# Sliding-window attention feeding an ELU feed-forward block on one core: x turned by DMA instead of by TensorE, and the attention pairs begun two steps sooner

## The chip, the core and the metric

The kernel runs on one core of a Trainium2 chip. The core has five engines with instruction streams of their own, and they meet only through semaphores: TensorE (PE, with its weight loads shown apart as PEld), VectorE (DVE), ScalarE (ACT), GpSimd (POOL) and SyncE (SP). Here SP does nothing but issue DMAs. The metric is device microseconds of one execution. A profiled execution has a span, from its first instruction to its last, which is a little shorter than its time.

## What is computed

```python
# attention, per batch b and head h: B=8, H=8, S=576, D=64
scores = scale * q @ k.T
scores = where(|i - j| <= 32, scores, -1e9)
attn   = exp(scores - max) / sum            # softmax over j
x      = attn @ v                           # -> (B*S, H*D) = (4608, 512)
# feed-forward, w_in (512, 2048), w_out (2048, 512)
h   = x @ w_in
g   = where(h > 0, h, exp(min(h, 0)) - 1)   # ELU
out = g @ w_out                             # (4608, 512)
```

## The kernel before

**Units of work.** The 4608 rows of x are cut into 36 pairs. A pair `i` is two blocks of 64 query rows, 128 rows in all, with all eight heads. Two pairs make a tile `t` of 256 rows for the feed-forward block, 18 tiles in all; pair `2t` is its first half, pair `2t+1` its second. The feed-forward work of a tile is eight steps of two slices of 128 hidden features each, so there are 144 steps, numbered `kk`. From the third tile on, tile `t` has steps 8t to 8t+7.

**A step.** The loop at the end of the kernel writes each step's work out in a fixed order, and each engine runs its own part of that order: `elu` of the step before (DVE, L446); the tasks in slot "dve"; `mm1` (eight PE matmuls, L433, the exponential on ACT, L439, and a subtraction on DVE, L441); the tasks in slot "mid"; `mm2` of two steps before (four PE matmuls, L460); the tasks in slot "end". After a tile's last step `mm2` also copies the result out of PSUM, half on ACT (L468) and half on DVE (L469), and stores it by SP (L470).

**A pair.** `pair_at(i, kk)` places the stages of one pair: `scores` (16 PE matmuls, L252, and an exponential on ACT, L258) in "mid" of step kk; `mask` (DVE, L267) and `pv` (16 PE matmuls, L279) in step kk+1; `normalize` (DVE, L288 and L291, which writes `x_st`) in "dve" of step kk+2 and `x_transpose` (four PE transposes into PSUM, L300) at its "end"; `x_evac` (DVE copy of PSUM to `xT`, L310) in "dve" of step kk+3. From pair 8 on kk is 4(i-2). So for the second half of tile t the four stages lie in steps 8t-4 to 8t-1, and `mm1` of step 8t, which reads both halves of `xT[t]`, comes next. Scores, attention output and transposed x share one PSUM buffer, tag "s".

**q, k and v.** For each batch b, SP loads q and k as f32 (`load_qk`, L109, 1152 KB each), POOL casts a quarter at a time (`cast_qk`, L207), PE transposes it (`transpose_qk`, L229, six transposes, PSUM tag "t0") and ACT copies it to `qT` or `kT` (L205). POOL loads v (`load_v`, L118), and SP makes a copy of it shifted by 64 rows with two DMAs (`rotate_v`, L124 and L125). The first step of the batch is `k0` = 4(9b//2 - 2). Batch 2 has its quarters transposed in steps 20 to 27, cast two steps ahead; a later batch has them in every second step from k0-15 on, cast five steps ahead. `rotate_v` is placed in step k0-4, the loads in steps k0-32 and k0-31 (not before 18), and `load_v` two steps after.

**Queues.** SP takes its DMAs strictly in the order of the loop, and one that has to wait keeps those behind it. The SP sequence is loads of q and k, shifts of v and stores of results. The pool of `xT` has three buffers, that of `x_st` two.

Of the kernel before, what the change touches and what calls it, by code (L numbers as in the profile page):

```python
# [10 lines left out]
BF16 = mybir.dt.bfloat16  # L11
# [10 lines left out]
def kernel(  # L22
# [9 lines left out]
    nc = tc.nc  # L32
# [11 lines left out]
    HP = H // 2  # L44
# [6 lines left out]
    TT = 256  # L51
    NT = N_TOK // TT
    NDO = D_MODEL // 128
# [3 lines left out]
    HALF = STEPS // 2  # L57
# [5 lines left out]
    wpool = ctx.enter_context(tc.tile_pool(name="weights", bufs=1))  # L63
    lpool = ctx.enter_context(tc.tile_pool(name="loads", bufs=2))
    apool = ctx.enter_context(tc.tile_pool(name="attn", bufs=2))
    xpool = ctx.enter_context(tc.tile_pool(name="xT", bufs=3))
    mpool = ctx.enter_context(tc.tile_pool(name="moe", bufs=3))
    opool = ctx.enter_context(tc.tile_pool(name="outs", bufs=2))

# [15 lines left out]
    def ps_tile(shape, dt, tag, name):  # L85
        return pools[tag].tile(shape, dt, tag=tag, name=name)
# [79 lines left out]
    for m in (1, 2, 0, 3, 4):  # L166
# [10 lines left out]
        out=masks, in_=masks, compare_op=ALU.is_ge, fill=0.0,  # L177
        base=0, pattern=[[0, 5], [-1, QB]], channel_multiplier=1)
    nc.gpsimd.affine_select(
        out=masks, in_=masks, compare_op=ALU.is_ge, fill=0.0,  # L180
        base=2 * WIN, pattern=[[0, 5], [1, QB]], channel_multiplier=-1)
    for mi in (0, 4):
        nc.gpsimd.affine_select(
            out=masks[:, mi, :], in_=masks[:, mi, :], compare_op=ALU.is_ge,
            fill=0.0, base=-WIN, pattern=[[0, QB]], channel_multiplier=1)
    nc.gpsimd.affine_select(
        out=masks[:, 3, :], in_=masks[:, 3, :], compare_op=ALU.is_ge,
# [55 lines left out]
    st = {}  # L243
# [59 lines left out]

    xT = {}

    def x_evac(i):
        t, z = i // 2, i % 2
        if z == 0:
            xT[t] = xpool.tile([128, NDO, TT], BF16, tag="xT", name="xT")
        nc.vector.tensor_copy(xT[t][:, :, z * 128:(z + 1) * 128], st.pop(i))  # L310

    def first_pair(b):
        return NQB * b // 2
# [20 lines left out]
    for fn in (pv, normalize, x_transpose, x_evac):  # L334
        for i in (0, 1):
            fn(i)
# [26 lines left out]
    def at(kk, slot, fn, *args):  # L363
        tasks.setdefault((kk, slot), []).append((fn, args))
# [5 lines left out]
    def pair_at(i, kk):  # L370
        at(kk, "mid", scores, i)
        at(kk + 1, "dve", mask, i)
        at(kk + 1, "end", pv, i)
        at(kk + 2, "dve", normalize, i)
        at(kk + 2, "end", x_transpose, i)
        at(kk + 3, "dve", x_evac, i)


    for i, tag in ((2, "s"), (3, "u")):
        at(0, "mid", scores, i, tag)  # L380
        at(1, "dve", mask, i)
        at(1, "mid", pv, i)
        at(2, "dve", normalize, i)
        at(2, "mid", x_transpose, i)
        at(3, "dve", x_evac, i)
# [11 lines left out]
    pair_at(6, 18)  # L397
    pair_at(7, 21)
    for i in range(8, NPAIR):
        pair_at(i, HALF * (i - 2))  # L400
    for b in range(2, B):
        k0 = HALF * (first_pair(b) - 2)
        for n in range(2 * HP):
            if b == 2:
                which, hp, kk, ahead = n // HP, n % HP, 20 + n, 2
            else:
                which, hp, kk, ahead = n % 2, n // 2, k0 - 15 + 2 * n, 5
            at(kk - ahead, "mid", cast_qk, b, which, WHOLE, (hp,), nc.gpsimd)
            at(kk, "mid", transpose_qk, b, which, WHOLE, (hp,), nc.scalar)
        at(k0 - HALF, "mid", rotate_v, b)  # L410
        if b >= 3:
            kk = max(k0 - 8 * HALF, 18)
            at(kk, "mid", load_qk, b, 0, WHOLE)
            at(kk + 1, "mid", load_qk, b, 1, WHOLE)
            for m in range(VS):
                at(kk + 2 + m // 3, "mid", load_v, b, m)
# [8 lines left out]
    def mm1(kk):  # L425
        t, s = order[kk]
        h = kk % 2 if kk < 18 else (kk + 2) % 3
        ps = ps_tile([128, FG, TT], FP32, f"h{h}", "ps")
        psH[kk] = ps
        for j in range(FG):  # L430
            fo = s * FG + j
            for do in range(NDO):
                nc.tensor.matmul(  # L433
                    ps[:, j, :],
                    lhsT=w_in_sb[:, do, fo * 128:(fo + 1) * 128],
                    rhs=xT[t][:, do, :],
                    start=(do == 0), stop=(do == NDO - 1))
        e_sb = mpool.tile([128, FG, TT], FP32, tag="e_sb")
        nc.scalar.activation(e_sb, ps, AX.Exp)  # L439
        m_sb = mpool.tile([128, FG, TT], BF16, tag="m_sb")  # L440
        nc.vector.tensor_scalar(m_sb, e_sb, -1.0, None, ALU.add)  # L441
        m_t[kk] = m_sb
# [30 lines left out]
    for kk in range(NSTEP + LAG):  # L473
        run(kk, "first")
        if 1 <= kk <= NSTEP:
            elu(kk - 1)
        run(kk, "dve")
        if kk < NSTEP:
            mm1(kk)
        run(kk, "mid")  # L480
        if kk >= LAG:
            mm2(kk - LAG)
        run(kk, "end")
# [30 lines left out]
```

## Time and profile before

| | |
|---|---|
| median of 3 runs | 351.5 us (351.49 to 351.5) |
| profiled execution, its own time | 352.11 us |
| its span | 350.4 us |
| PE busy | 314.8 us |
| DVE busy | 256.2 us |
| ACT busy | 167.2 us |
| POOL busy | 84.2 us |
| granted TensorE clock | 1.0 throughout |

Rows of the trace give a start and a length in us from the span's start, the engine, the line and the operation with its output and inputs. Where a row ends in brackets, it tells how long the engine was idle before it and what it waited for. Successive matmuls overlap in such rows, so the cost of a group of matmuls is read from one start to the next, not from the lengths.

### The profile page before, as it was taken

The numbers are of one execution on the slowest core, as the hardware profiler recorded it, in microseconds if no ns is written. First come the engines' busy times: TensorE is split into PE (matmuls) and PEld (weight loads), VectorE is DVE, ScalarE is ACT, GpSimd is POOL, SyncE is SP. The second block draws the span as 40 slices with busy tenths as digits, with TensorE's granted clock in tenths as the row PEclk, the third lists the DMA queues.
The fourth block names the chain that finished last, engine by engine and source line by source line (L and its number), as shares of the span: only waits on it lengthen the run. The fifth ranks groups of instructions, "written<-read, shape, count | busy, mean of one in ns | idle before, by whom it ended". The sixth has DMA issues, their size and how long they took to land.

```text
span 350.4 us, 8157 instructions
## 1 busy us (share of the span) xinstructions
PE 314.8 (90%) x3356; PEld 212.4 (61%) x3408; DVE 256.2 (73%) x474; ACT 167.2 (48%) x262; POOL 84.2 (24%) x108
## 2 busy tenths in 40 slices
PE   0347999688999999999999999999999999999994
PEld 0335666455666666666666566666666666666662
DVE  4456667786888777888777877778877777777763
ACT  2524273734645553545454554454545454444331
POOL 8432310282842304212601604031100000000000
PEclk9999999999999999999999999999999999999999
DMA  8999999999999739703939494950103010101011
GB/s 177 187 232 212 217 162 209 214 279 201 148 232 160 73 68 206 146 0 107 85 105 226 82 101 72 227 161 6 62 2 117 7 62 0 62 2 61 2 60 60
DMA packets 63944, 42.00 MB, mean 120 GB/s; under 512 B 38564, under 2 KB 58020, under 8 KB 63908
## 3 DMA queue, kind: packets, MB, share of 16 engines
q1 hardware_dynamic: 22180, 32.58, 38.8%
q0 software_dynamic: 41728, 8.92, 35.2%
q8 instruction: 26, 0.43, 0.5%
q14 instruction: 10, 0.08, 0.1%
HBM read 36.70 MB, written 9.44 MB: 132 GB/s over the span
## 4 chain that ended last, share of the span: by engine, by line
PE 73%; DVE 14%; ACT 4%; DMA 4%; issue 3%; SPq 0%; DVEq 0%
PE ps L433 32%; PE psY L460 28%; PE ptx L229 4%; DVE g_sb L446 4%; PE psS L252 3%; DVE x_st L291 3%; PE psXT L300 3%; PE psS L279 3%; ACT e_sb L439 3%; DVE m_sb L441 2%; DMA f<-in_k_dram 2%; DVE y_sb L469 2%; DMA Vo<-Ve 2%; DVE pm L267 2%; ACT pu L258 1%
## 5 line engine op out<-in xcount | busy, mean ns | idle before, releaser
L439 ACT ACTIVATE e_sb<-ps 128x512 f32<-128x512 f32 x144 | 86.0, 597 | 163.7 <-PE ps L433 163.6
L433 PE MATMUL ps<-xT,w_in_sb 128*128 128x256 bf16 x1152 | 150.7, 274 | 4.2 <-DVE xT L310 3.3
L460 PE MATMUL psY<-w_out_sb,g_sb 128*128 128x512 bf16 x524 | 141.0, 379 | 3.0 <-DVE g_sb L446 0.2
L433 PEld LDWEIGHTS <-w_in_sb 128*128 128x128 bf16 x1152 | 109.1, 98 | 34.7 <-issue 4.8
L441 DVE TENSOR_SCALAR m_sb<-e_sb 128x512 bf16<-128x512 f32 x144 | 72.0, 500 | 59.9 <-ACT e_sb L439 59.5
L446 DVE SCALAR_TENSOR_TENSOR g_sb<-ps,m_sb 128x512 bf16<-128x512 f32 x144 | 99.4, 690 | 13.0
L460 PEld LDWEIGHTS <-g_sb 128*128 128x128 bf16 x576 | 50.7, 97 | 38.0 <-DVE g_sb L446 0.7
L207 POOL CAST qkb<-f 96x768 bf16<-96x768 f32 x48 | 41.8, 889 | 110.1 <-DMA f<-in_q_dram 49.7
L118 POOL DMA_DIRECT2D Ve<-in_v_dram x40 | 34.1, 860 | 48.6 <-PE psS L279 34.6
L229 PE MATMUL ptx<-ident,qkb 96*128 96x96 bf16 x384 | 27.6, 215 | 14.5 <-DVE qkb L207 12.1
L258 ACT ACTIVATE pu<-psS 128x1024 bf16<-128x1024 f32 x36 | 36.4, 1018 | 1.8 <-PE psS L252 1.7
L229 PEld LDWEIGHTS <-qkb 96*128 96x128 bf16 x384 | 23.6, 102 | 16.8 <-DVE qkb L207 12.6
L267 DVE TENSOR_TENSOR pm<-pu,masks 128x1024 bf16<-128x1024 bf16 x36 | 27.8, 773 | 2.3 <-ACT pu L258 2.1
L291 DVE TENSOR_TENSOR x_st<-psS,rc 128x512 bf16<-128x512 f32 x36 | 24.9, 692 | 1.2
L279 PEld LDWEIGHTS <-pm 128*64 128x64 bf16 x576 | 12.5, 113 | 17.7 <-issue 8.1
L205 ACT COPY qT<-ptx 128x576 bf16<-128x576 bf16 (+1 forms) x30 | 20.0, 666 | 4.2 <-PE ptx L229 4.2
L300 PEld LDWEIGHTS <-x_st 128*128 128x128 bf16 x144 | 9.6, 99 | 16.5 <-DVE x_st L291 14.3
L300 PE MATMUL psXT<-ident,x_st 128*128 128x128 bf16 x144 | 14.6, 225 | 4.1 <-DVE x_st L291 3.6
L205 ACT COPY kT<-ptx 128x576 bf16<-128x576 bf16 (+1 forms) x26 | 17.4, 670 | 0.0
L279 PE MATMUL psS<-Ve,pm 128*64 128x65 bf16 x320 | 16.5, 200 | 0.6 <-ACT pu L258 0.3
L279 PE MATMUL psS<-Vo,pm 128*64 128x65 bf16 x256 | 14.5, 201 | 2.7 <-DMA Vo<-Ve 1.9
L252 PE MATMUL psS<-qT,kT 64*128 64x64 bf16 x576 | 15.3, 196 | 1.7 <-DVE xT L310 1.0
(29 smaller groups left out, 84.0 us busy)
## 6 DMA issues: line engine op xcount, KB each, us to landing
out_dram<-y_sb SPq DMA_DIRECT2D x18, 512.0 KB, 3.0
f<-in_q_dram SPq DMA_DIRECT2D x6, 1152.0 KB, 11.7
f<-in_k_dram SPq DMA_DIRECT2D x6, 1152.0 KB, 15.8
Vo<-Ve SPq DMA_DIRECT2D x12, 260.0 KB, 4.3
Ve<-in_v_dram POOLq DMA_DIRECT2D x24, 128.0 KB, 13.7
f<-in_q_dram SPq DMA_DIRECT2D x4, 576.0 KB, 9.6
f<-in_k_dram SPq DMA_DIRECT2D x4, 576.0 KB, 11.9
w_in_sb<-in_moe_w_in_dram POOLq DMA_DIRECT2D x4, 512.0 KB, 18.8
```

What stands on the lines that cost most here:

```text
L205: nc.scalar.copy(d_, s_)
L207: eng.tensor_copy(d_, s_)
L229: nc.tensor.transpose(pt[:, g, j * SP_:(j + 1) * SP_], src[:, j, g * 128:(g + 1) * 128], ident[0:SP_, 0:SP_])
L258: nc.scalar.activation(pu, _bap(psS, [psS.ap[0], [1, 1024]]), AX.Exp, scale=SCALE)
L267: nc.vector.tensor_mul(pm, pu, _bap(mm, [mm.ap[0], [0, H], [1, 2 * QB]]))
L279: nc.tensor.matmul(psS[QB * z:QB * (z + 1), par, hp * VD:(hp + 1) * VD], lhsT=pm[:, par * HP + hp, z * QB:(z + 1) * QB], rhs=vv[:, qb // 2 ...
L291: nc.vector.tensor_mul(x_st, _bap(psS, [psS.ap[0], [VD, HP], [512, 2], [1, D]]), _bap(rc, [rc.ap[0], [2, HP], [1, 2], [0, D]]))
L433: nc.tensor.matmul(ps[:, j, :], lhsT=w_in_sb[:, do, fo * 128:(fo + 1) * 128], rhs=xT[t][:, do, :], start=(do == 0), stop=(do == NDO - 1))
L439: nc.scalar.activation(e_sb, ps, AX.Exp)
L441: nc.vector.tensor_scalar(m_sb, e_sb, -1.0, None, ALU.add)
L446: nc.vector.scalar_tensor_tensor(g_sb, psH.pop(kk), 0.0, m_t.pop(kk), ALU.max, ALU.min)
L460: nc.tensor.matmul(psY[t][ts], lhsT=g_sb[:, j, ts * 128:(ts + 1) * 128], rhs=w_out_sb[:, s * FG + j, :], start=(s == 0 and j == 0), stop=( ...
```

## The change

From pair 8 on, x is no longer transposed by PE into PSUM and copied by DVE. `x_dma` has SP issue one transposing DMA, from `x_st` in SBUF to the pair's half of `xT` in SBUF, at the "end" of the step that normalizes. The layout of `xT` becomes (half, 128-column group, row), so that one half is a contiguous piece of 512 elements, and `mm1` reads its moving operand as two runs of 128. `xT` gets a fourth buffer. Pairs 9 and up start two steps sooner (pair 8 stays at step 24). The q and k transposes of batch 2 move from steps 20 to 27 to steps 18 to 25; those of a later batch lie in steps k0-16, k0-15, k0-12, k0-11, and so on. Pairs 0 to 7 keep PE and DVE.

```diff
-    xpool = ctx.enter_context(tc.tile_pool(name="xT", bufs=3))
+    xpool = ctx.enter_context(tc.tile_pool(name="xT", bufs=4))
...
-    def x_evac(i):
+    def xT_of(i):
         t, z = i // 2, i % 2
         if z == 0:
-            xT[t] = xpool.tile([128, NDO, TT], BF16, tag="xT", name="xT")
-        nc.vector.tensor_copy(xT[t][:, :, z * 128:(z + 1) * 128], st.pop(i))
+            xT[t] = xpool.tile([128, 2, NDO, 128], BF16, tag="xT", name="xT")
+        return xT[t][:, z, :, :]
+
+    def x_evac(i):
+        nc.vector.tensor_copy(xT_of(i), st.pop(i))
+
+    def x_dma(i):
+        x_st = st.pop(i)[3]
+        nc.sync.dma_start_transpose(
+            out=xT_of(i), in_=x_st.rearrange("p h d -> p (h d)"))
...
     for i in range(8, NPAIR):
-        pair_at(i, HALF * (i - 2))
+        kk = 24 if i == 8 else HALF * (i - 2) - 2
+        at(kk, "mid", scores, i)
+        at(kk + 1, "dve", mask, i)
+        at(kk + 1, "end", pv, i)
+        at(kk + 2, "dve", normalize, i)
+        at(kk + 2, "end", x_dma, i)
...
             if b == 2:
-                which, hp, kk, ahead = n // HP, n % HP, 20 + n, 2
+                which, hp, kk, ahead = n // HP, n % HP, 18 + n, 2
             else:
-                which, hp, kk, ahead = n % 2, n // 2, k0 - 15 + 2 * n, 5
+                which, hp = n % 2, n // 2
+                kk, ahead = k0 - 16 + HALF * hp + which, 5
...
-                    rhs=xT[t][:, do, :],
+                    rhs=xT[t][:, :, do, :],
```

## The prediction, made before the change was run

> **What bounds the kernel.** I read the page first (busy shares, slices, chain), then the waits, then the timeline of PE alone, step by step.
>
> ```profile
> span 350.4 us, 8157 instructions
> PE 314.8 (90%) x3356; PEld 212.4 (61%) x3408; DVE 256.2 (73%) x474; ACT 167.2 (48%) x262; POOL 84.2 (24%) x108
> PE   0347999688999999999999999999999999999994
> PE 73%; DVE 14%; ACT 4%; DMA 4%; issue 3%; SPq 0%; DVEq 0%
> ```
>
> PE is filled to nine tenths from the eleventh slice (about 88 us) to the end, so there the time is what PE has to do plus the holes in it. How much is which can be read from the starts of `mm1`, which opens each step. The first fence has four steps near the end, the second a step with a q or k transpose, the third the start of step 24.
>
> ```profile
> 319.65 1.04 PE L433 MATMUL ps<-xT,w_in_sb 128*128 128x256 bf16 x8
> 321.39 1.04 PE L433 MATMUL ps<-xT,w_in_sb 128*128 128x256 bf16 x8
> 322.36 0.41 PE L252 MATMUL psS<-qT,kT 64*128 64x64 bf16 x16
> 323.57 1.04 PE L433 MATMUL ps<-xT,w_in_sb 128*128 128x256 bf16 x8
> 325.79 1.05 PE L433 MATMUL ps<-xT,w_in_sb 128*128 128x256 bf16 x8
> 327.54 0.39 PE L300 MATMUL psXT<-ident,x_st 128*128 128x128 bf16 x4
> 327.76 1.04 PE L433 MATMUL ps<-xT,w_in_sb 128*128 128x256 bf16 x8
> 329.50 1.04 PE L433 MATMUL ps<-xT,w_in_sb 128*128 128x256 bf16 x8
> ```
>
> ```profile
> 208.15 1.04 PE L433 MATMUL ps<-xT,w_in_sb 128*128 128x256 bf16 x8
> 209.02 0.42 PE L229 MATMUL ptx<-ident,qkb 96*128 96x96 bf16 x6
> 210.14 1.04 PE L433 MATMUL ps<-xT,w_in_sb 128*128 128x256 bf16 x8
> ```
>
> ```profile
> 86.58 0.60 PE L433 MATMUL ps<-xT,w_in_sb 128*128 128x256 bf16 x4 [0.93 <-DVE xT L310]
> ```
>
> A bare step (319.65 to 321.39, 327.76 to 329.50) takes 1.74 us. With scores it takes 2.18 (321.39 to 323.57), so these cost 0.44; with `pv` 2.22 (to 325.79), so 0.48; with the x transposes 1.97 (to 327.76), so **0.23**; with a q or k transpose 1.99 (208.15 to 210.14), so 0.25. Steps 24 to 135, 112 of them, run from 86.58 to 329.50, 242.9 us. They hold 28 pairs and 44 q or k quarters: 112 x 1.74 + 28 x (0.44 + 0.48 + 0.23) + 44 x 0.25 = 194.9 + 32.2 + 11.0 = 238.1. So **4.8 us** are holes. Where they lie, the waits and one step show:
>
> ```profile
> PEld L300 <- DVE x_st L291: 14.3, 28, 1.1
> PE psXT L300 <- DVE x_st L291: 3.6, 9, 0.6
> ```
>
> ```profile
> 109.26 1.05 PE L433 MATMUL ps<-xT,w_in_sb 128*128 128x256 bf16 x8
> 109.47 0.68 DVE L469 COPY y_sb<-psY 128x512 f32<-128x512 f32 x1
> 110.06 0.68 DVE L446 SCALAR_TENSOR_TENSOR g_sb<-ps,m_sb 128x512 bf16<-128x512 f32 x1
> 110.66 0.19 DVE L288 RECIPROCAL rc<-psS 128x8 f32<-128x8 f32 x1
> 110.89 0.69 DVE L291 TENSOR_TENSOR x_st<-psS,rc 128x512 bf16<-128x512 f32 x1
> 111.64 0.40 PE L300 MATMUL psXT<-ident,x_st 128*128 128x128 bf16 x4 [0.46 <-DVE x_st L291]
> ```
>
> This step lasts from 109.26 to 111.87 where 1.97 is the work: DVE comes late because the store copy of L469 is ahead of it, and PE, which keeps its order, stands before the transposes. I put all 4.8 us to this place; that they are DVE's lateness and not the transposes' own is rival 2.
>
> **The change part by part.**
>
> *Removed from PE*: 28 groups of four transposes (pairs 8 to 35), 28 x 0.23 = 6.4 us, all on the path. *With them goes the wait for `x_st`*, up to 4.8 us. What is late next in that step is `mm2`, whose `g_sb` was made a step before, and after it `mm1`, whose `xT` is a step group old. Neither is near.
>
> *Removed from DVE and ACT*: 28 copies of L310.
>
> ```profile
> L310 DVE COPY xT<-psXT 128x512 bf16<-128x512 bf16 x36 | 14.9, 415 | 0.4 <-PE psXT L300 0.4
> ...
> L441 DVE TENSOR_SCALAR m_sb<-e_sb 128x512 bf16<-128x512 f32 x144 | 72.0, 500 | 59.9 <-ACT e_sb L439 59.5
> ...
> L267 DVE TENSOR_TENSOR pm<-pu,masks 128x1024 bf16<-128x1024 bf16 x36 | 27.8, 773 | 2.3 <-ACT pu L258 2.1
> ```
>
> 28 x 0.415 = 11.6 us of an engine that is 73% busy. In 8.4 us (four steps) DVE has 4 x (0.68 + 0.50) for ELU, 0.77 for the mask, 0.19 + 0.69 for normalizing and every other time 0.68 for the store: 6.4 to 7.1. So I count it at nothing beyond the holes. Counting steps modulo 4, the new order has normalizing in 0, the store copy in 1, scores in 2, `pv` in 3, and q or k transposes in 0 and 1. The store copy is no longer in the step ahead of normalizing.
>
> *Added to SP*: 28 transposing DMAs of 128 KB. The trace has no such DMA. For each, SP waits for `x_st`, and behind it wait loads, shifts and stores; loads have more than ten steps of lead, a store only frees `y_sb` two tiles later, and the shift of v (step k0-4, used at the end of k0-1) is issued after the x DMA of step k0-8, some seven steps (15 us) before its use.
>
> ```profile
> DMA  8999999999999739703939494950103010101011
> ```
>
> ```profile
> DMA to landing us min/median/max: 3.7/5.8/16.5
> DMA to landing us min/median/max: 3.2/9.2/24.6
> f<-in_q_dram SPq DMA_DIRECT2D x6, 1152.0 KB, 11.7
> f<-in_k_dram SPq DMA_DIRECT2D x6, 1152.0 KB, 15.8
> ```
>
> The slices show how busy the DMA engines are. Of the next four rows the first is the tile `Vo` (20 SBUF to SBUF copies, the nearest kin in size and route), the second `Ve` (40 loads of v, issued by POOL, 64 to 128 KB each). What the DMA may take before PE notices: the second half of tile t is normalized in step 8t-4 and read in 8t. The step and its `x_st`:
>
> ```profile
> 206.18 1.05 PE L433 MATMUL ps<-xT,w_in_sb 128*128 128x256 bf16 x8
> 206.78 0.69 DVE L291 TENSOR_TENSOR x_st<-psS,rc 128x512 bf16<-128x512 f32 x1
> ```
>
> `x_st` is ready 1.3 us into a step without a store copy. Four steps with two q or k transposes are 2 x 1.99 + 2.18 + 2.22 = 8.4 us, so the window is **7.1 us**; without them 7.9, so 6.6. A first half has four steps more. Bounds: 3.2 us at the shortest (hidden), 16.5 at the longest of the nearest kin (14 second halves x 9.6 = 135 us shown). No gain lies below nothing, since no step reads x sooner than 8t. I take about 4 to 6 us, by the `Vo` median: hidden.
>
> The Trainium skill ("VectorE: DVE Perf Modes", The three transpose paths) gives a 128x128 bf16 transpose 390 ns on TensorE and 1309 ns by the DMA crossbar, and its rules there choose TensorE where PSUM will do; that speaks against this change. By it four blocks one after the other are an estimated 5.2 us, still inside the window, so the sum would stay; the trace has no row for the crossbar, and its TensorE row shows four blocks in 0.40 us of PE's time.
>
> *`mm1`'s moving operand in two runs*: every moving operand in the trace is one run. Below: nothing. Above: no worse than two matmuls of 128 columns, 2 x 0.23/4 us against one of 256, 0.109 (eight from 208.15 to 209.02 above): 0.006 us x 1152 = 7 us. I take nothing, nearest to the 64-column score matmuls, 0.44/16 = 0.0275 us each, which already run at the same time per column.
>
> *Moved*: the q and k transposes keep their count, so their PE time stays; two of batch 2 go from after step 24 to before it, 0.5 us each way. Their casts were ready:
>
> ```profile
> 67.88 2.56 POOL L207 CAST qkb<-f 96x768 bf16<-96x768 f32 x3 [21.04 <-DMA f<-in_q_dram]
> 69.83 1.03 PE L433 MATMUL ps<-xT,w_in_sb 128*128 128x256 bf16 x8 [0.83 <-ACT y_sb L468]
> 73.00 1.68 DVE L267 TENSOR_TENSOR pm<-pu,masks 128x1024 bf16<-128x1024 bf16 x1
> 73.57 0.98 SPq L125 DMA_DIRECT2D Vo<-Ve  x1
> ```
>
> The first cast ends about 68.7 and step 18 starts at 69.83. The shift of v for batch 2 is issued by 74.5 and even with 16.5 us lands by 91; `pv` of pair 9, now in step 27, comes near 95. The steps up to 23 have holes of their own (this mask took 1.68 us where the mean is 0.77); I leave these as they are, with 1.5 us either way. The fourth buffer and the fuller dst copy of pairs 0 to 7 cost nothing on PE.
>
> **The sum**, against the profiled execution's own 352.1 us (span 350.4): 6.4 + 4.8 = 11.2 less; I give back 0.2 for the waits of 14 tiles on two DMAs each. 352.1 - 11.0 = 341.1; from the median 351.5, **340.5 us**.
>
> **Rivals.**
>
> 1. *Ring order behind the loads.* x goes through SP's queue with the loads. In steps 66 and 82 a load of q is issued right after a store, 2.6 steps (5.5 us) before the x DMA of pairs 19 and 23; the k loads of batches 4 and 5 go out 4 steps (8.4 us) before pairs 11 and 15. By the rows above they land 11.7 and 15.8 us after issue; x, another 3.7 after, would show 11.7 - 5.5 + 3.7 - 7.1 = 2.8 and 15.8 - 8.4 + 3.7 - 7.1 = 4.0, twice each: 13.6 us, 354. That is its ceiling, since those loads went out as pairs and the new order parts them by an x DMA; with half of it, **347**. The Trainium skill ("DMA: Bandwidth & Descriptors", Queues, rings and completion order) says that each DMA engine takes its descriptors in the order of the ring; the trace agrees in that the k load, issued just after q, lands 4 us later.
> 2. *The holes stay, elsewhere.* If PE only meets DVE's lateness at another place (`pm` before `pv`), the 6.4 us alone go: **345**. Against it: `pm` is made a full `mm1` and `mm2` ahead of `pv`.
> 3. *Slower: the transposing DMA is itself long.* If it is more like the loads of v, each of 14 second halves stops PE for what exceeds some 6.8 us. The gain is gone at 6.8 + 11.0/14 = **7.6 us** a DMA; with the `Ve` median 9.2 it is 14 x 2.4 = 34 us, **374 us**. For it: no row of such a DMA, and the DMA engines are 70% busy or more up to 123 us. Against it: the `Vo` copies of like size have a median below the window.
> 4. *Two runs cost their ceiling*: **347.5**.
>
> **Chances.** Forecast 0.60 (339 to 342); ring order 0.12 (342 to 354, of which 0.02 about even and 0.02 slower); holes stay 0.08; the DMA long 0.15; two runs 0.03; no net change by small things together 0.02. The range 339 to 349 leaves out rival 3 and the tail of rival 1, 0.19. Taking 0.2% as about what a measurement of this kernel can tell from no change: faster 0.60 + 0.08 + 0.08 + 0.03 = 0.79, same 0.04, slower 0.17.
>
> **What would show it.** Right: no L300 after the eighth pair; steps modulo 4 of 1.99, 1.99, 2.18, 2.22 on PE from step 24 on; no row in which PE waits for a DMA of `xT`; these DMAs landing within 6 us. Rival 1: such waits at steps 40, 56, 72 and 88 alone. Rival 2: longer waits of L279 for `pm`. Rival 3: a wait at the first `mm1` of nearly every tile from 32 on. Rival 4: bare steps above 1.74 and L433 starts more than 0.109 apart. I am wrong if x DMAs take more than 7 us where the other DMAs are idle.

## The result

| | before | after |
|---|---|---|
| median | 351.5 us | 341.65 us |
| profiled execution / its span | 352.11 / 350.4 us | 341.63 / 339.9 us |
| ratio, 95% interval | | 0.9725, 0.9708 to 0.9742 |

Forecast were 340.5 us and a range of 339 to 349. Ratios here and below compare fast runs alone; two of the ten runs of the experiment with both loads ahead were slow, over 1.5% above its fastest. The page of the changed kernel, in the rows that answer to those shown of before (PE's slices and busy shares, the chain by engine, the x DMAs among the issues):

```profile
span 339.9 us, 8051 instructions
...
PE 308.7 (91%) x3296; PEld 207.4 (61%) x3296; DVE 246.2 (72%) x446; ACT 167.3 (49%) x262; POOL 84.3 (25%) x108
...
PE   0347999799799999999999999999999999999994
...
PE 83%; DVE 7%; DMA 4%; ACT 3%; issue 1%; SPq 0%; DVEq 0%
```

```profile
xT<-x_st SPq DMA_TRANSPOSE x28, 3.4
```

DVE's share of the chain has gone from 14% to 7%, PE's from 73% to 83%. The profile of the tile `xT` tells how long SP's sequencer is held by one transposing DMA (1.19 us) and how long they take from issue to landing:

```profile
L317 SPq DMA_TRANSPOSE xT<-x_st x28: 1189/1191/1549, 93.4 to 313.9; - x28
...
DMA to landing us min/median/max: 2.4/3.4/6.4
```

PE's timeline has bare steps and one with scores and one with `pv` (row 310.07 to 312.29) late in the span; the second fence has one step with a q or k transpose, at the start of tile 9:

```profile
304.41 1.05 PE L447 MATMUL ps<-xT,w_in_sb 128*128 128x256 bf16 x8
...
306.16 1.04 PE L447 MATMUL ps<-xT,w_in_sb 128*128 128x256 bf16 x8
...
307.89 1.04 PE L447 MATMUL ps<-xT,w_in_sb 128*128 128x256 bf16 x8
...
310.07 1.04 PE L447 MATMUL ps<-xT,w_in_sb 128*128 128x256 bf16 x8
...
312.29 1.05 PE L447 MATMUL ps<-xT,w_in_sb 128*128 128x256 bf16 x8
```

```profile
188.68 1.05 PE L447 MATMUL ps<-xT,w_in_sb 128*128 128x256 bf16 x8
...
190.68 1.04 PE L447 MATMUL ps<-xT,w_in_sb 128*128 128x256 bf16 x8
```

They take 1.75, 1.73, 2.18, 2.22 and 2.00 us; the forecast had 1.74, 1.74, 2.18, 2.22 and 1.99. No row of the waits names PE waiting for a DMA of `xT`. Steps 87 and 91 are longer by 0.2 and 0.1 us. But one step is far off, step 26:

```profile
91.15 1.05 PE L447 MATMUL ps<-xT,w_in_sb 128*128 128x256 bf16 x8
...
92.68 0.69 DVE L291 TENSOR_TENSOR x_st<-psS,rc 128x512 bf16<-128x512 f32 x1
...
93.43 0.41 PE L252 MATMUL psS<-qT,kT 64*128 64x64 bf16 x16 [1.23 <-DVE x_st L291]
...
94.64 1.04 PE L447 MATMUL ps<-xT,w_in_sb 128*128 128x256 bf16 x8
```

It lasts 3.49 us where a step with scores takes 2.18. Scores wait for `x_st` of the pair before, because both use PSUM buffer "s": pair 8 stayed at step 24 while pair 9 moved to 26, so pair 9 starts in the step in which pair 8 is normalized.

Steps 24 to 135 run from 86.24 to 319.25, 233.0 us against 242.9. That is 9.9 of the 10.5 us by which the spans differ.

### The profile page after: what moved, and what is told of

Read it like the earlier page. It is cut to its first block, busy times and chain, and to the rows that moved or that the text cites. A ratio compares the mean times of both kernels' runs of the same rounds, so it can differ in the third digit from the quotient of the medians.

```text
span 339.9 us, 8051 instructions
## 1 busy us (share of the span) xinstructions
PE 308.7 (91%) x3296; PEld 207.4 (61%) x3296; DVE 246.2 (72%) x446; ACT 167.3 (49%) x262; POOL 84.3 (25%) x108
## 4 chain that ended last, share of the span: by engine, by line
PE 83%; DVE 7%; DMA 4%; ACT 3%; issue 1%; SPq 0%; DVEq 0%
PE ps L447 36%; PE psY L474 35%; PE ptx L229 5%; PE psS L279 4%; PE psS L252 3%; DMA f<-in_k_dram 2%; DVE g_sb L460 2%; DMA Vo<-Ve 2%; DVE m_sb L455 1%; ACT e_sb L453 1%; DVE x_st L291 1%; ACT pu L258 1%; ACT qkb L205 1%; DVE pm L267 1%; DVE xT L313 1%
## 5 line engine op out<-in xcount | busy, mean ns | idle before, releaser
L474 PE MATMUL psY<-w_out_sb,g_sb 128*128 128x512 bf16 x576 | 148.0, 379 | 0.2 <-DVE g_sb L460 0.2
L118 POOL DMA_DIRECT2D Ve<-in_v_dram x40 | 34.8, 875 | 28.1 <-PE psS L279 13.6
L267 DVE TENSOR_TENSOR pm<-pu,masks 128x1024 bf16<-128x1024 bf16 x36 | 26.0, 721 | 2.0 <-ACT pu L258 1.7
L279 PEld LDWEIGHTS <-pm 128*64 128x64 bf16 x576 | 12.5, 113 | 17.3 <-DVE pm L267 13.4
L252 PEld LDWEIGHTS <-kT 64*128 64x128 bf16 x576 | 11.2, 98 | 10.2 <-issue 7.7
L483 DVE COPY y_sb<-psY 128x512 f32<-128x512 f32 x18 | 12.4, 687 | 2.2 <-PE psY L474 1.8
## 6 DMA issues: line engine op xcount, KB each, us to landing
Ve<-in_v_dram POOLq DMA_DIRECT2D x24, 128.0 KB, 10.9
```

Of the source, the lines that this page charges most:

```text
L118: nc.gpsimd.dma_start(out=V_e[b % 3][p0:p1, m, :, 0:D], in_=v[b, :, lo + p0:lo + p1, :].rearrange("h p d -> p h d"))
L252: nc.tensor.matmul(psS[:, h % 2, hp * 128 + z * QB:hp * 128 + (z + 1) * QB], lhsT=kT[b % 2][base:base + 64, hp, QB * qb:QB * qb + 128], rh ...
L279: nc.tensor.matmul(psS[QB * z:QB * (z + 1), par, hp * VD:(hp + 1) * VD], lhsT=pm[:, par * HP + hp, z * QB:(z + 1) * QB], rhs=vv[:, qb // 2 ...
L474: nc.tensor.matmul(psY[t][ts], lhsT=g_sb[:, j, ts * 128:(ts + 1) * 128], rhs=w_out_sb[:, s * FG + j, :], start=(s == 0 and j == 0), stop=( ...
```

## The experiments

Ratios below are to the kernel before. All kernels compute the whole result. An edit is shown against the changed kernel or, where the text puts pair 9 in step 27, against the kernel of the first experiment. The rows are again of `mm1` starts, of PE's waits and of landings.

**Pair 9 in step 27.**

```diff
-        kk = 24 if i == 8 else HALF * (i - 2) - 2
+        kk = {8: 24, 9: 27}.get(i, HALF * (i - 2) - 2)
```

> The changed kernel with pair 9 started in step 27 instead of 26, all else the same. Step 26 of the changed kernel took 3.49 us where a step with scores takes 2.18: pair 8 stayed at step 24, so its x_st and the scores of pair 9, which share one PSUM buffer, fall in one step. Theory A: this is a hole that the change itself made, and it goes: 1.3 us less, about 340.3 us; step 27 then takes 2.18. Rival: the hole is one that DVE's lateness makes in any case and moves on to step 28 or 29: 341.6 us.

Measured 340.03 us, ratio 0.9683 (0.9657 to 0.971), the fastest kernel of the study. Steps 26, 27 and 28 start here:

```profile
91.00 1.05 PE L447 MATMUL ps<-xT,w_in_sb 128*128 128x256 bf16 x8
...
92.75 1.04 PE L447 MATMUL ps<-xT,w_in_sb 128*128 128x256 bf16 x8
...
94.93 1.04 PE L447 MATMUL ps<-xT,w_in_sb 128*128 128x256 bf16 x8
```

Step 26 is bare (1.75), step 27 has the scores (2.18), and nothing moved on: theory A. Steps 24 to 135 take 231.4 us, 1.6 less than in the changed kernel.

**The old starting steps, with DMA.**

```diff
-        kk = 24 if i == 8 else HALF * (i - 2) - 2
+        kk = HALF * (i - 2)
```

> The changed kernel with the pairs from 9 on started where they were before, at steps 4(i-2), so without the two steps. The window from x_st of a second half to the first matmul of its tile falls from 7.1 us to 2 x 1.74 - 1.3 = 2.2 us. Theory A: the DMAs take as long as in the changed kernel (issue to last landing 2.3 to 6.4 us, 53 us over the 14 second halves), so PE stops for what exceeds 2.2, about 15 to 22 us in all, less the 1.3 us of step 26: 355 to 362 us, slower than before. Rival: the two steps are not needed because the landing is late only on paper, or the gain came from the new order of the steps: 340 us or 345 us.

Measured 365.54 us, ratio 1.0405 (1.0357 to 1.0454). All 14 tiles wait:

```profile
PE ps L447 <- DMA xT<-x_st: 19.1, 14, 5.6
```

So the two steps are what hides the DMA. The time is above the range expected, though the waits are inside it: after the two long waits (5.6 us the longest) steps 72 and 88 took 1.9 and 1.4 us more than their work. The section on the hardware comes back to that.

**PE transposes, at the new places.**

```diff
-        kk = 24 if i == 8 else HALF * (i - 2) - 2
-        at(kk, "mid", scores, i)
-        at(kk + 1, "dve", mask, i)
-        at(kk + 1, "end", pv, i)
-        at(kk + 2, "dve", normalize, i)
-        at(kk + 2, "end", x_dma, i)
+        pair_at(i, {8: 24, 9: 27}.get(i, HALF * (i - 2) - 2))
```

> The kernel with PE transposes and DVE copies as before, but with the new places: pairs 8 and 9 at steps 24 and 27, the later ones two steps sooner than before, and the q and k transposes where the change put them. Theory A: the 6.4 us of transposing stay, and most of the 4.8 us of holes go, since the store copy no longer stands ahead of normalizing; step 30 may wait for the copy of pair 9: 346.5 to 348 us. Rival 1: the holes belong to waiting for x_st at the end of a step and stay: 351 us. Rival 2: nearly all of the gain comes from the places: 342 us.

Measured 348.01 us, ratio 0.9907 (0.9877 to 0.9937): theory A, at its upper end. In steps 24 to 135 the trace has 1.6 us of holes instead of 4.7, all in steps 26, 27 and 30, around the pair that was set between two rhythms; from step 31 on, where normalizing no longer follows a store copy, none is left. So the change is two things: the new places took some 3.5 us, and on top of them the DMA took 8.0 (348.01 to 340.03). This split holds for that order only, because the DMA alone removes the same holes. In the run with the old starting steps normalizing still follows a store copy, but PE has no transposes there and does not wait; step 34, 2.61 us in the kernel before, starts and ends here:

```profile
107.74 1.05 PE L447 MATMUL ps<-xT,w_in_sb 128*128 128x256 bf16 x8
...
109.49 1.04 PE L447 MATMUL ps<-xT,w_in_sb 128*128 128x256 bf16 x8
```

It takes 1.75 us, a bare step, and so do the thirteen others from 26 to 130 that normalize behind a store copy.

**PE's work without its waits.** With pair 9 in step 27: beside each x DMA stand four PE transposes of the identity into the pair's PSUM buffer, which nobody reads.

```diff
-        x_st = st.pop(i)[3]
+        x_st, tag = st.pop(i)[3:]
+        pt = ps_tile([128, NDO, 128], BF16, tag, "psXT")
+        for do in range(NDO):
+            nc.tensor.transpose(pt[:, do, :], ident, ident)
```

> The kernel with pair 9 at step 27, and beside each x DMA four PE transposes of the identity matrix into the PSUM buffer of the pair, which nobody reads: PE's work of the transposes comes back without their wait for x_st and without the DVE copy. Theory A: PE is the bound in these steps, so 28 x 0.23 = 6.4 us come back: 340.0 + 6.4 = 346.4 us. Rival: PE's time for them was hidden in its weight loads and only waits were removed: 340 us.

Measured 348.98 us, ratio 0.9921 (0.989 to 0.9952): 8.95 more than without them, not 6.4. A step with them:

```profile
246.60 0.39 PE L319 MATMUL psXT<-ident 128*128 128x128 bf16 x4
246.83 1.04 PE L450 MATMUL ps<-xT,w_in_sb 128*128 128x256 bf16 x8
...
248.82 1.04 PE L450 MATMUL ps<-xT,w_in_sb 128*128 128x256 bf16 x8
```

The transposes start 0.23 us before the next step, as before, and each of the 28 steps is longer by this 0.23: the 6.4 us are confirmed. Steps 24 to 135 take 7.5 us more: besides the 6.4, step 26 loses 0.9 us, where these transposes wait for their buffer. The rest of the profiled difference, 2.3 us, lies before step 24, 1.7 of it in steps 16 and 17, whose program is the same in both kernels. There the granted clock stood at half for 3.4 us (the section on the hardware has the rows). That is no price of the transposes, and it makes this median uncertain by about that much.

DVE's 28 copies cost nothing that shows: with them, at the same places, steps 24 to 135 took 239.3 us, without them and with the same PE work 239.0.

**Both loads ahead of the x DMA.**

```diff
-            at(kk + 1, "mid", load_qk, b, 1, WHOLE)
+            at(kk, "mid", load_qk, b, 1, WHOLE)
```

> The changed kernel with the load of k placed in the same step as that of q, so that SP issues both together ahead of the x DMA, as it did in the kernel before. In the changed kernel the x DMAs of pairs 19 and 23, each behind one load of 1152 KB, landed 6.4 and 6.1 us after issue, 0.4 and 0.9 us before PE needed them. Theory A: SP's transfers go in the order of the queue; with two loads ahead, which landed some 16 us after issue as a pair, these two x DMAs land about 4 to 5 us too late, and PE waits for them at the start of steps 72 and 88: 8 to 10 us, about 350 us. Rival: transfers share the DMA engines evenly and a small one overtakes a large one: 341.6 us, no such waits.

Measured 353.23 us (352.8 for the eight runs that the ratio uses), ratio 1.0042 (1.0018 to 1.0066): one line gives the whole gain back. The waits are the two expected ones, at tiles 9 and 11:

```profile
PE ps L447 <- DMA xT<-x_st: 7.2, 2, 4.2
```

They are 3.0 and 4.2 us; the loss is 11.1 us (352.8 against 341.65), again more than the waits. Why the changed kernel escapes this is seen in its SP rows for the same place:

```profile
177.33 0.41 SPq L109 DMA_DIRECT2D f<-in_q_dram  x1
181.87 1.19 SPq L317 DMA_TRANSPOSE xT<-x_st  x1
183.15 0.53 SPq L109 DMA_DIRECT2D f<-in_k_dram  x1
```

The x DMA waits for its `x_st` and holds SP meanwhile, so the k load leaves 5.8 us after the q load instead of half a microsecond.

**One step sooner instead of two.**

```diff
-        kk = 24 if i == 8 else HALF * (i - 2) - 2
+        kk = 24 if i == 8 else HALF * (i - 2) - 1
```

> The changed kernel with the pairs from 9 on one step sooner than before the change instead of two. The window of a second half falls to about 1.99 + 1.74 + 2.18 - 1.3 = 4.6 us. The landings of the changed kernel were over 4.6 us for pairs 9, 17, 19, 21 and 23 (4.8, 5.3, 6.4, 4.9, 6.1), 4.5 us in all; step 26 has no hole. Theory A: waits of 0.2 to 2 us at those five tiles alone and about 344 us. Rival: as with no step sooner, nearly every tile waits: over 350 us. In the two runs with long waits PE lost more than it waited for; waits below 2 us will show whether that depends on their length: if not, about 347 us.

Measured 357.58 us, ratio 1.0175 (1.0139 to 1.0211). My expectation missed an order: one step later, the x DMAs of pairs 19 and 23 stand behind both loads in SP's program, so these two landed 9.2 and 10.0 us after issue. Five tiles wait, 11.6 us in all: those of pairs 9, 17, 19 and 23, as named, and of 13 in place of 21. The waits below 1 us cost about what they last (steps 47 and 63 are 0.8 and 1.0 us longer, and those after them are normal); the two long ones cost 2.3 us each on top.

**The x DMAs on a queue of their own**, with pair 9 in step 27.

```diff
-        nc.sync.dma_start_transpose(
+        nc.scalar.dma_start_transpose(
```

> The kernel with pair 9 at step 27, and the x DMAs issued by ACT, on a queue of their own, instead of SP. Theory A: x DMAs were late where loads were ahead of them in SP's order, so those of pairs 19 and 23 land in 3 to 4 us after issue instead of 6.2 and 6.3; the time stays, 340.0 us, since none was late enough to be seen, and ACT, half idle, has room for 1.2 us of issuing a pair. Rival: they are late because the DMA engines are shared with whatever else runs: still about 6 us. If issuing delays ACT's exponential, the time grows by up to some 0.3 us a pair, 348 us.

Measured 369.36 us, ratio 1.0499 (1.0448 to 1.055), far from both. Four tiles wait, those of pairs 9, 13, 19 and 23, for 4 to 5 us each (the first row). SP, now free, sends both loads at once (the other two):

```profile
PE ps L447 <- DMA xT<-x_st: 17.7, 4, 4.8
...
190.38 0.39 SPq L109 DMA_DIRECT2D f<-in_q_dram  x1
190.88 0.95 SPq L109 DMA_DIRECT2D f<-in_k_dram  x1
```

Here the k load lands at 205.35, and the x DMA of pair 19, issued by ACT at 194.91 on another queue, at 205.59. It is the same at pair 13 (148.7 and 149.0). So theory A's premise is wrong: a queue of its own does not let x past the loads. A new theory (B): an x DMA lands behind all loads issued before it, on whichever queue. The same trace narrows this to what SP has issued: the x DMA of pair 9 landed at 109.8, 0.7 us behind SP's k load, but 0.8 to 2.6 us ahead of three loads of v that POOL had issued 4 to 7 us before it.

**The same, with the loads apart.** As the last, with the k loads of batches 4 to 7 behind the next store.

```diff
-            at(kk + 1, "mid", load_qk, b, 1, WHOLE)
+            at(kk + (0, 0, 0, 1, 2, 2, 6, 6)[b], "mid", load_qk, b, 1, WHOLE)
```

> The kernel whose x DMAs are issued by ACT, with the k loads of batches 4 to 7 placed two to six steps later, behind the next store, so that SP issues one load at a time, as it does when x DMAs stand between them. With both loads in flight an x DMA on ACT's queue landed 0.3 to 0.8 us after the second load, as it did on SP's. Theory B: an x DMA lands behind every load issued before it, on whichever queue, so what keeps it in time is that SP, held by x, issues the second load late: with the loads apart the x DMAs of pairs 13, 19 and 23 land in at most about 6.5 us and the time is about 340 to 342 us. Rival: ACT's queue serves the x DMAs worse than SP's: they stay at 9 us or more in those places and the time over 355 us.

Measured 349.4 us, ratio 0.9934 (0.9903 to 0.9966). The landings are as B has them for the pairs named but for pair 23 (7.1), and the time follows neither theory: pairs 11, 21 and 25 now have a k load and two shifts of v ahead of them, and with pair 23 they hold PE for 0.2 to 1.0 us each; pair 9 holds it for 2.6. These waits come to 5.1 us; the rest of the loss was not taken apart.

**The loads behind the x DMA.** On SP, with pair 9 in step 27.

```diff
-            kk = max(k0 - 8 * HALF, 18)
+            kk = {3: 18, 6: 72, 7: 88}.get(b, k0 - 8 * HALF)
```

> The kernel with pair 9 at step 27, and the loads of batches 6 and 7 placed four steps later, so that they follow the x DMAs of pairs 19 and 23 instead of preceding them. Theory B: those two x DMAs, 6.2 and 6.3 us before, land in 3 to 4 us; nobody waited for them, so the time stays at 340.0 us. Rival: what is moved comes late in its turn (a load for its cast, or an x DMA elsewhere), and the time grows by 1 us or more.

Measured 341.64 us (340.37 to 344.53), ratio 0.9737 (0.9702 to 0.9771), against 340.03 (339.91 to 341.18) without this edit. The two landings fell, to 3.3 and 4.7 us (3 to 4 were expected), and steps 24 to 135 take 231.8 us in its profile (231.4 without the edit); a longer stretch lies in steps 18 to 23, which the edit does not touch. No gain, and whether the median is really higher is open.

Issue to last landing in us, from the landing records of the traces, for the second halves in question:

| x DMA of pair | changed kernel | pair 9 in step 27 | both loads ahead | one step sooner | ACT's queue | ACT, loads apart | loads behind |
|---|---|---|---|---|---|---|---|
| 13 | 2.7 | 2.7 | 2.6 | 4.7 | 10.9 | 6.3 | 2.6 |
| 19 | 6.4 | 6.2 | 9.7 | 9.2 | 10.7 | 6.1 | 3.3 |
| 23 | 6.1 | 6.3 | 10.9 | 10.0 | 11.0 | 7.1 | 4.7 |

**Pair 6 by DMA too**, with pair 9 in step 27 and loads moved out of its way.

```diff
-    pair_at(6, 18)
     pair_at(7, 21)
-    for i in range(8, NPAIR):
-        kk = {8: 24, 9: 27}.get(i, HALF * (i - 2) - 2)
+    for i in (6, *range(8, NPAIR)):
+        kk = {6: 18, 8: 24, 9: 27}.get(i, HALF * (i - 2) - 2)
...
-            kk = max(k0 - 8 * HALF, 18)
+            kk = {3: 18, 6: 72, 7: 88}.get(b, k0 - 8 * HALF)
             at(kk, "mid", load_qk, b, 0, WHOLE)
-            at(kk + 1, "mid", load_qk, b, 1, WHOLE)
+            at(21 if b == 3 else kk + 1, "mid", load_qk, b, 1, WHOLE)
```

> The kernel with pair 9 at step 27, with pair 6 transposed by DMA too, the k load of batch 3 placed behind it (step 21 instead of 19), and the loads of batches 6 and 7 four steps later, so that they follow the x DMAs of pairs 19 and 23 instead of preceding them. Theory A: 0.23 us of PE and the wait of pair 7's scores for the copy of pair 6 (0.58 us in step 21) go: 339.2 us; the DMAs of pairs 19 and 23 land in 3 to 4 us. Rival: the DMA of pair 6, in the busiest stretch, lands after step 24 starts and PE waits: 341 us or more.

Measured 341.81 us, ratio 0.9721 (0.9695 to 0.9747). The DMA of pair 6 took 7.3 us and landed as step 24 began, and the hole in step 21 went (0.58 to 0.14); but pair 9's DMA now comes late and PE waits for it:

```profile
PE ps L446 <- DMA xT<-x_st: 2.6, 2, 1.6
```

The longest, 1.6 us at step 32, is pair 9's. The other, 0.9 us at step 24, is in every kernel here, where PE waits for the copy of pair 7. Against the kernel with the loads behind (341.64) pair 6's DMA gains nothing. The edit also puts the k load of batch 3 two steps later, and which of the two made pair 9's DMA late was not separated.

## Why the prediction was right, and where it was off

**The bound and the 6.4 us** were right. The steps came out within 0.02 us of the forecast, and 28 x 0.23 us came back step by step when idle transposes were put in.

**The 4.8 us of holes** were DVE's lateness and not the transposes' own: with PE transposes at the new places 1.6 us were left. Either part of the change removes them: at the new places no store copy stands ahead of normalizing, and the DMA takes away the PE work that waited. The prediction's cause, that the wait goes with the transposes, is therefore right but not the only one. Rival 2 falls: the weight loads of `pv` waited longer for `pm` (13.4 us in 30 waits, 7.4 in 15 before), but the steps with `pv` stayed at 2.21 to 2.22 us from step 27 on, except 87 and 91.

**The term that was missed** is step 26, 1.3 us. The prediction priced what was moved by its count ("the q and k transposes keep their count") and did not ask who shares PSUM buffer "s" where the old rhythm meets the new: pair 9 moved, pair 8 did not. With 11.0 - 1.3 = 9.7 us it would have given 341.8. Moving pair 9 by one step showed it. The early steps 18 to 23, left "1.5 us either way", gave 0.8 us, though two quarters' 0.5 us came into them; that this makes up for part of step 26 is luck.

**The hidden DMA** was right in kind. In size it was taken too large (4 to 6 us, where the median is 3.4 and the range 2.4 to 6.4), which cost nothing, since all of it was hidden. That all would land within 6 us was wrong for pairs 19 and 23. Their slack was 0.4 and 0.9 us.

**Rival 1, ring order**, did not come but was near, and its mechanism was not quite what the prediction took. Its ceiling for pairs 19 and 23 was 11.7 - 5.5 + 3.7 = 9.9 us; they took 6.4 and 6.1 because the order parts the loads, as the prediction said. With both loads ahead they took 9.7 and 10.9, and the kernel 353 us. But the order of SP's ring is not the cause, or not the only one, since x on ACT's queue was as late.

**Rival 3** did not come: no x DMA of the changed kernel was over 6.4 us. Its price, that PE stops for what exceeds the window, is too low for long waits: with the old starting steps the waits were 19.1 us, and steps 72 and 88 lost 3.3 more. **Rival 4** falls with the bare steps of 1.74 us. DVE's copies counted at nothing: confirmed within what the runs can tell.

## What to carry to other kernels

When work is taken off a full engine, price it by the start-to-start time of that engine's steps; here this gave every step from 27 on to 0.02 us, except two that lost 0.1 and 0.2 us. A transfer in its place is free while it lands inside its window: count what is in flight when it is issued, and remember that an in-order queue that waits can be what keeps large transfers apart. Where some items of a pipeline are moved and others stay, look at the seam: the last one that stays and the first that moves share every buffer of which there is only one.

## What the runs showed of the hardware

**A wait of PE can cost more than it lasts.** In the run with both loads ahead, PE waited 2.97 us at the start of step 72, and after it the same eight matmuls took 1.58 us, half as long again as usual (1.04):

```profile
191.53 1.58 PE L447 MATMUL ps<-xT,w_in_sb 128*128 128x256 bf16 x8 [2.97 <-DMA xT<-x_st]
...
195.09 1.13 PE L447 MATMUL ps<-xT,w_in_sb 128*128 128x256 bf16 x8
```

The windows of that run before, after and past this stretch, with the granted clock right after the five engines' busy times:

```profile
186.30:191.50 5.20, 2.21 (x28) 1.40 (x28) 3.21 (x6) 0.98 (x2) 1.01 (x2) 1.00 0.97 177
191.50:195.10 3.60, 3.57 (x19) 2.16 (x20) 1.22 (x2) 1.13 (x2) 3.60 (x5) 0.55 0.16 28
195.10:197.10 2.00, 1.94 (x18) 1.47 (x18) 0.74 (x2) 0.84 (x2) 1.92 (x3) 0.96 1.41 90
```

The clock falls to 0.55 for 3.6 us. In the run one step sooner it stood at 0.50 for 6.8 us, of which 5.1 lay behind the wait of pair 19. The length of the wait alone does not settle whether this happens. A wait of 1.93 us (before step 40 of the run with the old starting steps) left the next step at its full speed; one of 2.64 us (before step 32 with the loads apart on ACT's queue) made the next 1.6 us longer. With the idle transposes PE waited 1.86 us before step 16 and the clock halved; in the kernel without them it waited 1.85 us there and kept its clock. The windows of these two, in this order:

```profile
66.40:69.80 3.40, 3.40 (x19) 1.87 (x16) 1.70 (x3) 1.99 (x3) 1.46 (x2) 0.50 1.11 217
66.40:69.80 3.40, 2.85 (x27) 1.87 (x26) 2.54 (x5) 3.27 (x5) 0.66 (x1) 1.00 1.10 224
```

The Trainium skill ("TensorE: Matmul & The Clock Gate", Part 1) has the clock halve after an idle window of about 3.4 us and come back after as long a busy one. The factor agrees with the trace (0.50), and so do the lengths of the slow stretches (3.4 and 6.8 us); but here it halved after waits as short as 1.86 us.

**A transposing DMA is held up by loads on another queue.** In the run with the x DMAs on ACT's queue, pair 19's is issued at 194.91 with two loads on SP's queue ahead of it. The DMA view gives packets, MB and a share by queue; the packets matter here. SP's queue is q1 and ACT's q10. The first row is from 194.91 to 201.1, the other two from 201.5 to 203:

```profile
q1 hardware_dynamic: 896, 1.35, 107.4%
...
q1 hardware_dynamic: 154, 0.24, 110.3%
q10 hardware_dynamic: 161, 0.04, 29.5%
```

In the first 6.2 us no packet of ACT's queue moved; for pair 27, with nothing else in flight, the first moved 1.2 us after issue. From then on the two queues moved about packet for packet, and the x DMA landed 0.2 us behind the second load. The Trainium skill ("DMA: Bandwidth & Descriptors", Queues, rings and completion order) says that a DMA engine takes turns between queues, packet by packet. The second stretch agrees with that, 154 packets to 161. What kept back the first packet no run here shows, nor whether the transposing or the second queue makes it so, since no plain DMA was put in its place.
